# Transposing P by DMA instead of on TensorE in a two-layer recurrent attention and SwiGLU kernel

## The chip, the core and the metric

The kernel runs on one core of a Trainium2 chip. The metric is the device time of one execution in microseconds, taken over several runs as a median. Beside the runs stands one profiled execution, whose trace gives the start and length of every instruction and DMA on the core.

## What is computed

Four blocks run one after another on x (2048 x 576, bfloat16), with the same weights in both layers:

```python
x = x + A(layernorm(x)); x = x + B(layernorm(x))
x = x + A(layernorm(x)); x = x + B(layernorm(x))

def A(x, mem0, Wq, Wk, Wv, Wo, seg_len):      # 32 heads of 128, M = 8, seg_len = 32
    mem = mem0
    for s in range(n_seg):                     # 64 segments, one after another
        h = concatenate([mem, xs])             # 8 + 32 = 40 rows
        q, k, v = h @ Wq, h @ Wk, h @ Wv
        p = softmax(where(mask, q @ k.T * scale, -1e9))
        o = (p @ v) @ Wo
        mem = o[:, :M]; outs.append(o[:, M:])
    return concatenate(outs)

def B(x, w1, w3, w2):                          # 576 -> 4608 -> 576
    return (silu(x @ w1) * (x @ w3)) @ w2
```

Each segment needs the memory rows that the segment before it produced, so A is a chain of 64 steps.

## The kernel before

The two layers are interleaved: step t works on segment t of the first layer and segment t - 8 of the second (LAG = 8). There are 72 steps. The first and last eight have one layer only; the 56 between have both, and there the columns of both layers (2 x 40 = 80) go through TensorE together. The feed-forward part runs on groups of four segments, 18 weight blocks to a group, between the instructions of the attention.

A step has four groups of eight heads. A group's path is: QK and its tail QKt (queries and keys into PSUM, copied out to the tile QKT), SC (scores), the softmax on VectorE and ScalarE (add the mask, row maximum, subtract, exp, sum, reciprocal) in the tile SME, sm_pb (line 1000), which writes the normalised P into the tile PB, TR (ptr, line 1015), which transposes P of eight heads by eight matmuls against a selection matrix into two PSUM banks, PTe (pt_ev, line 1027), which copies the two banks into the tile PTS on ScalarE or VectorE, PV (line 1033), which multiplies V with PTS, an eviction into the tile OT, and WO with its tail WOt. PB has two buffers, PTS one. After a transpose GpSimd clears PB (pb_zero, line 1009), since sm_pb writes only parts of it. With both layers PB holds 104 rows (first layer in rows 0 to 39, second in 64 to 103).

The order of the work is made when the program is built. make_nodes (line 232) creates nodes with an engine, a duration, dependencies and the buffers that they take and free. plan (line 76) then places them. TensorE's order is written out by hand in strings of letters: ORDER = FIRST + FOUR * 11 + LAST, where FOUR is four steps with both layers. For the other engines plan takes, at each moment, the ready node that can start first, and among these the one with the lowest prio. A node of engine "DMA" goes to SP's queue (lines 599 to 600), "SWD" to GpSimd's, and "AD" to ScalarE or VectorE, whichever is free first. Each engine issues in exactly this order.

The letters: Q and q are QK and QKt, S is SC, T is TR, P is PV, O and o are WO and WOt, F and f the feed-forward's up-projection and its tail, W and w its down-projection for the two layers, G and g the value projection of a group and its tail, V, v, X, x other value projections, n, a and b the transposes behind the layer norms, p the transpose of the attention's output, m that of the first memory.

Each TensorE node also has tiling modes in which it can run: "full" (128 x 128), "col" (the weights in two halves of 64 columns, side by side), "row" (64 rows, two side by side) and a few smaller ones. A node with "full/col" runs in whichever of the two is set. plan adds SWITCH to a node that changes the mode. In "col" the helper mm (line 586) splits each matmul into two halves.

The weights of the feed-forward come from memory for each group anew: W13 (four DMAs, shown as tile W) and W2C (one DMA), each with two buffers, all from SP's queue. The layer norms write the normalised rows into XN, with the last 64 columns a second time behind them, so that five whole 128-column blocks can be transposed (ln_tr, line 774).

All TensorE instructions are recorded under line 591, ScalarE's under 594, VectorE's under 597 and SP's DMAs under 600, because helpers issue them.

Of the kernel before, what the change touches and what calls it, by code (L numbers as in the profile page):

```python
# [29 lines left out]
R_HT = 6  # L30

SWITCH = 0.098
# [43 lines left out]
def plan(nodes, pools, letters):  # L76
# [42 lines left out]
    while len(order) < len(nodes):  # L119
# [74 lines left out]
def ewh(*ns):  # L194
# [5 lines left out]
    "amQQQQqqqqSSqqQQQTSQqqSxXVvPTPTOPOOTooPoOoQQqqqqQSQvqqSVQQqTqSQPQOSToPXTOPTxoPOOooQqqqQQSVvqQQSQqqqQSqTQPOSTPTOP"  # L200
    "OToooPaOoQQqqqqQQSvSVQqqqQQQSqTPSXTOPTOPoTxoPOOooQQpQqqqvVqSnQQSFfqFQqfqqQTQSPFTfSOFPWOToPFToffPOOooWQqqqqQQSQQS"
    "FFfqfVvqTQWQqSFxffqQFPSXTWfPFTOPOTOPFOooooWQfqqqQQSFqfqVvQQSFfqTQPWQSqqfFTQOSfoPFTOPWFTOPooffOoFQqqQqqvSQQWSVqqf"
    "FQQWqqSTQPQSTOPabOTXPooTOPxxOooXqqpQQQqqSQnVvfSFTQqqqQQPSFffqQFTOPoSWTFfPOOTFPWOooofQQqfqqFSQFqqfgQGWTQPQSfqFQQq"
    "fqFSWTGFSggfGPGTOPOTfgFaPOOooooWVvqqfQQFFQSqfqQWQSqqfFQTQQqfqSFPWTSFPOTfoOPFWTOPffFOoooWQQqqqqQSbQQQqgqSGSTGPQTq"
    "gqQPOggSGTGPOTOPoooOoQqqqpQVpSQnQvqqqQnQFSTffqFQQPqSwTFPSffOOWTFPFTOPWOoooowFffqqQQQWSfqqFQwQSFqfqgGTQQPWfqSTFFg"
    "gfqGQwPGTOoSPFgfOGTOPWOoooFqqfqQQQQvSwqVSFqqfQQWwTFPQfqfqFTQSwPWSfFOTFPWwOTffFPOOaooooWQQqqqqQwSbQGQgqqSQTQPQqqg"
    "SGTSGPGggTOPOTOPoooOo"
# [5 lines left out]
LAST = (  # L213
    "QqqqpQQQSnpQQqqqVSvTSnQFffqPFOQqTwPoSWTFPffFTOOWPwOoooFFqfqQQQqqfSQQwQfqqFTSGSqfgQFPWQgfqGTSFPGFTfggOOPGTOPwWOoo"
    "ooFFqffqQQwQWQSqqVSvqqQQTFQPSfqqQwTOWSPFTFPofOTOPwOoooWFfqfqQQQQqfqSFwWvVSFTfqqQQPWQqqSvTQVSPOTbOPwOTooPoxOoXqQp"
    "pVvQqqqQSQQnqqSQnqQFTSfqQPFTSOPfTFOPwTOPWOooooFqfqfQQQSVqqqvQQQwSfqFWTFPSfqqQTQOPSFTwfFPOTOPWOooooFfqqQQQSqfxvVX"
    "qfFQwWTSQFQqqqfQPWSTwFPffqQFTWSOwFPffOFTOPwOooooWFvqfqQQQSWqqVQwSFfqqfQFTQQSqqWPQTPSOoTOPwOToobPxOoXqqqQQQpvSVqQ"
    "qQSnqQFfSTQFPqqfQOTSFfPwTOoofPFTOPFOfoowQqqQFSQfqqqQQSVvqqfQFTQFSfqPQOTowPSFTfxXPOTOPFOooowVvqqQQQSqqfQQSqqfQFST"
    "QQPwqqFTSOfPFTOfPwTOPfoooOoFQQqqqqQSQQSqqQVvSfTFPqQQwqfTSFPOTOFPTOPfoooOoFpwnfffFFwFwfffFFFwfffFFwFwfffFFFwfffFF"
    "wFwfffFFFfww"  # L220
# [11 lines left out]
def make_nodes(em, nseg, pools, o=Opt, dma_bw=230e3, load_bw=400e3):  # L232
# [44 lines left out]
    def ln_nodes(tag, src, xn, deps, prio, writes, warm=False):  # L277

        a = node("DVE", 1.16, em.ln_stats(src, xn), deps=deps, prio=prio, acq=[] if src is xn else [xn], name=tag + "stats")
        p_ = node("POOL", 0.45, em.ln_pow(xn), deps=[a], prio=prio, name=tag + "pow")  # L280
        c = node("DVE", 0.46 if src is xn else 0.66, em.ln_norm(src, xn), deps=[p_], prio=prio, name=tag + "norm")
        b = Slot("bank", users=len(writes))
        d = node("PE", 5 * 0.056, em.ln_tr(xn, b, warm), deps=[c], prio=prio, mode="full/col", acq=[b], rel=[xn], name=tag + "tr")
# [26 lines left out]
    def v_nodes(name, t, k, prio, tail_at, emit, strips, deps, tail_deps, free):  # L310
# [3 lines left out]
        m_ = node("PE", 8 * 0.2158, emit(b, False), deps=deps, prio=prio, mode=modes[0], acq=b, name=name)  # L314
# [40 lines left out]
    def step(t):  # L355
# [17 lines left out]
        for g in range(NG):  # L373
# [30 lines left out]
            pe_ = [node("AD", ew(4 * c80), em.pt_ev(t, g, m, bt[m], pts), deps=[tr], prio=pf, rel=[bt[m]], name="PTe") for m in (0, 1)]  # L404
# [163 lines left out]
class Emitter:  # L568
# [116 lines left out]
    def load_xn(self, g, xn):  # L685
        return lambda n: (self.dma if g else self.adma)(self.T.XN[:, xn.i, 0:D], self.a.x[g * P:(g + 1) * P, :])
# [52 lines left out]
    def init_mem(self, li, t):  # L739
        co = M_AT[self.kind(t, li), role(t)]  # L740
        return lambda n: self.v("tensor_copy", self.ht(t)[:, :, co:co + MEM], self.T.mem0T[:])


    def src_ap(self, src):
        return self.T.XN[:, src.i, 0:D] if src.pool == "xn" else self.T.XR[:, src.i, :]
# [17 lines left out]
    def ln_norm(self, src, xn):  # L763
        def f(n):
            L = self.T.LNS[:, xn.i]
            self.v("tensor_scalar", self.T.XN[:, xn.i, 0:D], self.src_ap(src), L[:, 12:13], L[:, 15:16],
                   op0=ALU.subtract, op1=ALU.mult)
            self.v("tensor_copy", self.T.XN[:, xn.i, D:D + R64], self.T.XN[:, xn.i, D - R64:D])
# [245 lines left out]

    def ptr(self, t, g, pb, b):

        def f(n):
            nq = self.nq(t)
            e = role(t) if nq == SW else 0
            sel = self.T.ident[0:104, R64 * e:R64 * e + QW]  # L1020
            if nq == SW:
                sel = bass.AP(sel.tensor, sel.offset, [list(v) for v in sel.ap][:1] + [[R64, 2], [1, QW]])
            for j in range(GH):
                self.mm(self.bk(b[j // 4])[:, (j % 4) * nq:(j % 4 + 1) * nq], self.T.PB[0:104, pb.i, j, :], sel, True, True)
        return f

    def pt_ev(self, t, g, m, b, pts):
        def f(n):
            w = 4 * self.nq(t)
            self.cp(n, self.T.PTS[:, pts.i, m * w:(m + 1) * w], self.bk(b)[:, 0:w])  # L1030
# [162 lines left out]
    def fin_cast(self, xr, xn):  # L1193
        return lambda n: self.act(self.T.XN[:, xn.i, 0:D], self.T.XR[:, xr.i, :], ACT.Copy)

    def store(self, g, xn, last):
        return lambda n: (self.dma if last else self.swdma)(self.a.out[g * P:(g + 1) * P, :], self.T.XN[:, xn.i, 0:D])
# [7 lines left out]
def kernel(  # L1205
# [39 lines left out]
    T.ident = sp.tile([P, P + QW], BF, name="ident")  # L1245
# [5 lines left out]
    T.mem0T = sp.tile([P, 5, MEM], BF, name="mem0T")  # L1251
# [12 lines left out]
    T.YTS = sp.tile([P, 2, 5, P], BF, name="YTS")  # L1264
    T.W13 = sp.tile([P, pools["w13"], NCH, 2 * P], BF, name="W13")
# [10 lines left out]
    nc.gpsimd.tensor_copy(T.ident[:, P:P + QW], T.ident[:, 0:QW])  # L1276
# [55 lines left out]
```

## Time and profile before

| | us |
|---|---|
| median of 3 runs | 2678.95 (2677.48 to 2689.47) |
| span of the profiled execution | 2684.2 |
| of it TensorE / VectorE / ScalarE / GpSimd busy | 2621.2 / 2111.8 / 1346.4 / 332.2 |
| one period FOUR (four steps) in the middle | 156.35 |

The profiled execution's own time is its span, from the first to the last instruction; nothing of it outside the span is recorded. It lies 5.2 us above the median of the runs. Matmuls overlap in TensorE, so the length of one (about 200 ns for 80 columns) is not its price; the distance from the start of one group of matmuls to the start of the next is.

### The profile page before, as it was taken

The page shows a single profiled execution, that of the slowest core. Times are in us where ns is not written, and L with a number is a line of the kernel's source. Part 1 is how long each engine was busy: PE and PEld are TensorE (multiplying, and loading weights), DVE is VectorE, ACT ScalarE, POOL GpSimd, SP SyncE. Part 2 cuts the span into 40 slices and gives each one's busy share as a digit, 9 for nine tenths or more (in the row PEclk, how much of TensorE's full clock was granted, in tenths as well). Part 3 has the DMA queues.
Part 4 walks back from the last instruction along what each step waited for, and adds up shares of the span by engine and source line. Part 5 has one row for each costly group of instructions (what it writes and reads, how often), then busy time and mean ns, then how long its engine had stood idle before and what let it go on. Part 6 is the DMA issues. An engine that isn't in the chain of part 4 may idle for free.

```text
span 2684.2 us, 136846 instructions
## 1 busy us (share of the span) xinstructions
PE 2621.2 (98%) x60881; PEld 2292.9 (85%) x60933; DVE 2111.8 (79%) x5485; ACT 1346.4 (50%) x3916; POOL 332.2 (12%) x400
## 2 busy tenths in 40 slices
PE   5999999999999999999999999999999999999998
PEld 4888888889888888988888898888889888888887
DVE  4787887887888778787877878787787878687876
ACT  2655554454545455454544545454454545455453
POOL 1111110110111011011101101110110111011110
PEclk8999999999999999999999999999999999999999
DMA  9064524344342434434333443423344342334457
GB/s 319 4 178 118 166 72 125 97 120 118 99 127 84 114 99 119 118 100 126 88 112 97 120 118 100 126 87 113 98 120 118 102 126 82 114 98 130 125 169 256
DMA packets 478178, 322.08 MB, mean 120 GB/s; under 512 B 26024, under 2 KB 467760, under 8 KB 476944
## 3 DMA queue, kind: packets, MB, share of 16 engines
q1 hardware_dynamic: 474048, 305.43, 38.7%
q8 instruction: 477, 7.82, 1.2%
q0 software_dynamic: 3024, 6.93, 0.9%
q10 hardware_dynamic: 512, 0.94, 0.2%
q14 instruction: 117, 0.96, 0.1%
HBM read 308.49 MB, written 2.36 MB: 116 GB/s over the span
## 4 chain that ended last, share of the span: by engine, by line
PE 89%; DMA 3%; DVE 3%; ACT 3%; issue 1%; SPq 1%; ACTq 0%; DVEq 0%
PE bank L591 89%; ACT V L594 1%; SPq L600 1%; DMA W<-in_B_w_dram 1%; DMA W<-in_A_Wk_dram 1%; DVE STAT L597 1%; DVE SME L597 0%; DMA WO<-in_A_Wo_dram 0%; DVE V L597 0%; DVE HTT L597 0%; DVE PB L597 0%; DMA XN<-in_A_x_dram 0%; ACT SME L594 0%; DVE PTS L597 0%; ACT PTS L594 0%
## 5 line engine op out<-in xcount | busy, mean ns | idle before, releaser
L591 PEld LDWEIGHTS <-W 128*128 128x128 bf16 (+2 forms) x32064 | 1267.3, 100 | 118.8 <-issue 55.7
L591 PE MATMUL bank<-HT,W 128*128 128x80 bf16 (+3 forms) x23040 | 807.0, 197 | 14.9 <-ACT HT L594 5.7
L591 PE MATMUL bank<-XTB,W 128*64 128x256 bf16 (+5 forms) x9024 | 664.3, 263 | 4.6 <-DMA W<-in_B_w_dram 3.1
L594 ACT ACTIVATE QKT<-bank 128x256 bf16<-128x256 f32 (+2 forms) x1477 | 343.2, 314 | 362.1 <-PE bank L591 334.1
L1010 POOL MEMSET PB<- 128x1024 bf16 x288 | 273.9, 951 | 1888.4 <-PE bank L591 1537.4
L591 PE MATMUL bank<-OT,WO 128*128 128x80 bf16 (+3 forms) x11520 | 410.9, 198 | 4.6 <-issue 2.0
L591 PEld LDWEIGHTS <-WO 128*128 128x128 bf16 (+1 forms) x11520 | 381.4, 102 | 30.4 <-issue 17.7
L594 ACT ACTIVATE V<-bank 32x512 bf16<-32x512 f32 (+1 forms) x594 | 335.8, 585 | 110.9 <-PE bank L591 104.5
L591 PE MATMUL bank<-WV,HT 128*32 128x512 bf16 (+4 forms) x3628 | 366.2, 383 | 5.5 <-issue 3.2
L591 PE MATMUL bank<-W2C,HTT 128*64 128x288 bf16 (+1 forms) x3040 | 320.1, 287 | 0.8 <-DMA W2C<-in_B_w_dram 0.4
L597 DVE TENSOR_REDUCE STAT<-SME 104x8 f32<-104x320 f32 (+1 forms) x576 | 274.6, 477 | 18.2 <-ACT SME L594 12.4
L597 DVE TENSOR_TENSOR PB<-SME,STAT 40x128 bf16<-40x128 f32 (+4 forms) x912 | 274.9, 335 | 11.3 <-POOL PB L1010 0.5
L594 ACT ACTIVATE HTT<-bank 128x512 bf16<-128x512 f32 (+1 forms) x324 | 177.6, 557 | 196.8 <-PE bank L591 195.5
L591 PEld LDWEIGHTS <-HT 128*32 128x32 bf16 (+4 forms) x3680 | 158.1, 99 | 120.3 <-issue 17.9
L591 PEld LDWEIGHTS <-HTT 128*64 128x64 bf16 (+1 forms) x3104 | 229.4, 104 | 32.1 <-issue 0.6
L597 DVE CAST QKT<-bank 128x128 bf16<-128x128 f32 (+4 forms) x571 | 154.5, 317 | 123.4 <-PE bank L591 122.4
L597 DVE SCALAR_TENSOR_TENSOR XR<-bank,XR 128x288 f32<-128x288 f32 x576 | 239.6, 446 | 13.8 <-PE bank L591 10.9
L597 DVE SCALAR_TENSOR_TENSOR HTT<-HTT,bank 128x512 bf16<-128x512 bf16 (+1 forms) x324 | 202.1, 624 | 56.1 <-ACT HTT L594 51.8
L594 ACT ACTIVATE OT<-bank 128x320 bf16<-128x320 f32 (+1 forms) x425 | 157.0, 405 | 169.5 <-PE bank L591 165.5
L597 DVE TENSOR_TENSOR HTT<-HTT,bank 128x512 bf16<-128x512 bf16 (+1 forms) x324 | 203.6, 628 | 29.0 <-PE bank L591 1.4
L594 ACT ACTIVATE PTS<-bank 128x320 bf16<-128x320 f32 (+1 forms) x395 | 148.2, 404 | 132.3 <-PE bank L591 95.7
L594 ACT ACTIVATE SME<-SME 104x320 f32<-104x320 f32 (+1 forms) x288 | 135.3, 470 | 153.4 <-DVE SME L597 151.1
(61 smaller groups left out, 1837.7 us busy)
## 6 DMA issues: line engine op xcount, KB each, us to landing
W<-in_B_w_dram SPq DMA_DIRECT2D x612, 256.0 KB, 3.7
W2C<-in_B_w_dram SPq DMA_DIRECT2D x306, 288.0 KB, 3.3
W<-in_B_w_dram SPq DMA_DIRECT2D x612, 32.0 KB, 3.3
W<-in_B_w_dram SPq DMA_DIRECT2D x8, 1024.0 KB, 10.5
W<-in_A_Wq_dram SPq DMA_DIRECT2D x9, 512.0 KB, 9.7
WO<-in_A_Wo_dram SPq DMA_DIRECT2D x4, 1152.0 KB, 17.7
XR<-in_A_x_dram POOLq DMA_DIRECT2D x16, 288.0 KB, 3.4
WV<-in_B_w_dram SPq DMA_DIRECT2D x4, 1152.0 KB, 11.3
```

Source lines behind the costliest of these rows:

```text
L591: self.ch("PE", self.nc.tensor.matmul(out, lhsT=lhsT, rhs=rhs, start=start, stop=stop, skip_group_check=True, **k))
L594: self.ch("ACT", self.nc.scalar.activation(*a, **k))
L597: self.ch("DVE", getattr(self.nc.vector, fn_)(*a, **k))
L600: self.ch("SP", self.nc.sync.dma_start(out=out, in_=in_))
L1010: return lambda n: self.ch("POOL", self.nc.gpsimd.memset(self.T.PB[:, pb.i], 0.0))
```

## The change

- In the steps with both layers, TR is no longer eight matmuls and two copies. It is one DMA that transposes rows 0 to 111 of PB (PTR = 112) for eight heads into PTS, issued from SP's queue. The planner counts 1.25 us in the queue and 1.7 us until the result can be used. PTS is laid out for 112 columns a head, and PV picks its 80 columns out of it.
- In the steps with one layer, TR stays on TensorE.
- The transposes behind the layer norms take two column halves each (mode "col" only); the second copy of the last 64 columns and its VectorE instruction are gone. XN, ident and mem0T take less memory.
- The three strings are new, and plan has a price for each pair of modes.

```diff
+PTR = 112
-SWITCH = 0.098
+SWITCH = 0.1
+SWITCHES = {"full col": 0.104, "full row": 0.107, "row full": 0.105, "row col": 0.106, "col full": 0.128, "col row": 0.14}
@@ plan
-                dur += SWITCH
+                dur += SWITCHES.get(f"{mode[0]} {n.mode[0]}", SWITCH) if mode else SWITCH
@@ FIRST, LAST: other strings
...
 FOUR = (
-    "QvqqpQQpQqqVSSnnQQFqfqfFQTQfqqWSFPwTFPSfOOTFPwTOPWOooooFffqqQQQQqqSWFSFffqgGQTQPQQgqqqGSwTFPGSfgfgFTGOPOWTOPwOoo"
-    "ooFqqQQQQqfqVvSSwWFfqfqQQTFWQwQSFffqqFPWTOPSowTFPffOTOFPWwOoooFqqfqQQQWQSqqqaQSQQbQqgqSGTSGPgTGPOTggOPGTOPwOoooo"
+    "QQppQqqqqQvVSnnSQFqqfqQQFSqffQPFwOSPWFoffPOFOWwPFOoooFfqfqQQQQqqSWGSFqqfgQQQPQgqqwSGSFPGffggFWGPOwOFPOOoooowVqfq"
+    "vQQQQqfqWSFSFfqqqQQwWQFPfqfSFwQOPSWFoFPffOOWPwOoooFqqfQQWQSqqqQQaSbQQqgqqGSQgPGSGPGggOPOwOPoooOo"
 )
@@ make_nodes, ln_nodes
-        c = node("DVE", 0.46 if src is xn else 0.66, em.ln_norm(src, xn), ...
+        c = node("DVE", 0.43 if src is xn else 0.6, em.ln_norm(src, xn), ...
-        d = node("PE", 5 * 0.056, em.ln_tr(xn, b, warm), ..., mode="full/col", ...
+        d = node("PE", 5 * 0.056, em.ln_tr(xn, b, warm), ..., mode="col", ...
@@ make_nodes, step
-            bt = banks()
-            tr = node("PE", 8 * mm80, em.ptr(t, g, pb, bt), deps=[pbs], prio=pf + o.tr, mode="full/col", acq=[pts] + bt, name="TR")
+            if nl == 2:
+                tr = node("DMA", 1.25, em.ptr_dma(t, g, pb, pts), deps=[pbs], prio=pf - 0.02, acq=[pts], name="TR", lat=1.7)
+            else:
+                bt = banks()
+                tr = node("PE", 8 * mm80, em.ptr(t, g, pb, bt), deps=[pbs], prio=pf + o.tr, mode="full/col", acq=[pts] + bt, name="TR")
             node("POOL", 1.2, em.pb_zero(pb), deps=[tr], prio=pf, rel=[pb], name="pbz")
-            pe_ = [node("AD", ew(4 * c80), em.pt_ev(t, g, m, bt[m], pts), ...) for m in (0, 1)]
+            pe_ = [tr] if nl == 2 else [node("AD", ew(4 * c80), em.pt_ev(t, g, m, bt[m], pts), ...) for m in (0, 1)]
@@ Emitter
     def ln_norm(self, src, xn):
...
-            self.v("tensor_copy", self.T.XN[:, xn.i, D:D + R64], self.T.XN[:, xn.i, D - R64:D])
     def ln_tr(self, xn, b, warm=False):
...
             for c in range(5):
-                self.mm(self.lnps(b)[:, c, :], self.T.XN[:, xn.i, c * P:(c + 1) * P], self.T.ident[:, 0:P], True, True, is_transpose=True)
+                for r in (0, R64):
+                    c0 = min(c * P + r, D - R64)
+                    self.mm(self.lnps(b)[r:r + R64, c, :], self.T.XN[:, xn.i, c0:c0 + R64], self.T.ident[:, 0:P], True, True,
+                            is_transpose=True, tile_position=(0, r))
+    def ptr_dma(self, t, g, pb, pts):
+        def f(n):
+            e, q = ("SP", self.nc.sync) if n.by == "DMA" else ("ACT", self.nc.scalar)
+            self.ch(e, q.dma_start_transpose(out=self.T.PTS[:, pts.i], in_=self.T.PB[0:PTR, pb.i].rearrange("p h n -> p (h n)")))
+        return f
     def pv(self, t, g, pts, b):
         def f(n):
             nq = self.nq(t)
+            e = role(t)
             for j in range(GH):
+                if nq == SW:
+                    x = self.T.PTS[:, pts.i, j, R64 * e:R64 * e + QW]
+                    x = bass.AP(x.tensor, x.offset, [list(v) for v in x.ap][:1] + [[R64 * (1 - 2 * e), 2], [1, QW]])
+                else:
+                    x = self.T.PTS[:, pts.i].rearrange("p h q -> p (h q)")[:, j * QW:(j + 1) * QW]
                 self.mm(self.bk(b[j // 4])[...], self.T.V[...],
-                        self.T.PTS[:, pts.i, j * nq:(j + 1) * nq], True, True)
+                        x, True, True)
@@ tiles
-    T.XN = sp.tile([P, pools["xn"], D + R64], BF, name="XN")
+    T.XN = sp.tile([P, pools["xn"], D], BF, name="XN")
-    T.PTS = sp.tile([P, pools["pts"], GH * 2 * QW], BF, name="PTS")
+    T.PTS = sp.tile([P, pools["pts"], GH, PTR], BF, name="PTS")
...
```

More of the change, by code (lines that the diff above doesn't have):

```diff
@@ L280, in ln_nodes @@
         p_ = node("POOL", 0.45, em.ln_pow(xn), deps=[a], prio=prio, name=tag + "pow")
-        c = node("DVE", 0.46 if src is xn else 0.66, em.ln_norm(src, xn), deps=[p_], prio=prio, name=tag + "norm")
+        c = node("DVE", 0.43 if src is xn else 0.6, em.ln_norm(src, xn), deps=[p_], prio=prio, name=tag + "norm")
         b = Slot("bank", users=len(writes))
-        d = node("PE", 5 * 0.056, em.ln_tr(xn, b, warm), deps=[c], prio=prio, mode="full/col", acq=[b], rel=[xn], name=tag + "tr")
+        d = node("PE", 5 * 0.056, em.ln_tr(xn, b, warm), deps=[c], prio=prio, mode="col", acq=[b], rel=[xn], name=tag + "tr")
         out = []
@@ L313, in v_nodes @@
         b = banks()
-        m_ = node("PE", 8 * 0.2158, emit(b, False), deps=deps, prio=prio, mode=modes[0], acq=b, name=name)
+        m_ = node("PE", 8 * 0.2158 + 0.11, emit(b, False), deps=deps, prio=prio, mode=modes[0], acq=b, name=name)
         n = node("PE", 0.2158, emit(b, True), deps=deps + tail_deps, prio=prio + tail_at, mode=modes[1], acq=b, name=name + "t")
@@ L1028, in f @@
         def f(n):
[L1029 to L1030 removed]
+            w = 4 * QW
+            self.cp(n, self.T.PTS[:, pts.i].rearrange("p h q -> p (h q)")[:, m * w:(m + 1) * w], self.bk(b)[:, 0:w])
         return f
@@ L1193, in fin_cast @@
     def fin_cast(self, xr, xn):
-        return lambda n: self.act(self.T.XN[:, xn.i, 0:D], self.T.XR[:, xr.i, :], ACT.Copy)
+        return lambda n: self.act(self.T.XN[:, xn.i, :], self.T.XR[:, xr.i, :], ACT.Copy)
     def store(self, g, xn, last):
-        return lambda n: (self.dma if last else self.swdma)(self.a.out[g * P:(g + 1) * P, :], self.T.XN[:, xn.i, 0:D])
+        return lambda n: (self.dma if last else self.swdma)(self.a.out[g * P:(g + 1) * P, :], self.T.XN[:, xn.i, :])
 class Tiles:
@@ L1243 @@
     T.WO = wp.tile([P, H, D], BF, name="WO")
-    T.ident = sp.tile([P, P + QW], BF, name="ident")
+    T.ident = sp.tile([P, P], BF, name="ident")
     T.maskb = sp.tile([P, 2, QW], BF, name="maskb")
```

48 lines of the change are left out of this document (20 added, 28 removed).

## The prediction

> **What bounds the kernel now.** I read the page first: span, busy times, chain.
>
> ```profile
> span 2684.2 us, 136846 instructions
> PE 2621.2 (98%) x60881; PEld 2292.9 (85%) x60933; DVE 2111.8 (79%) x5485; ACT 1346.4 (50%) x3916; POOL 332.2 (12%) x400
> ...
> PE 89%; DMA 3%; DVE 3%; ACT 3%; issue 1%; SPq 1%; ACTq 0%; DVEq 0%
> ```
>
> TensorE is busy 98% of the span and carries 89% of the chain that ended last. The program repeats one string of letters, FOUR, eleven times, so next come the stretches of one period (four steps with both layers).
>
> ```profile
> 1155.43:1311.78 156.35, 155.62 (x3468) 137.45 (x3472) 125.12 (x323) 79.16 (x229) 18.53 (x23) 1.00 0.38 109
> ...
> 1286.00:1296.00 10.00, 10.00 (x271) 9.07 (x269) 9.31 (x29) 5.85 (x26) 0.55 (x1) 1.00 0.02 4
> 1296.00:1306.00 10.00, 9.82 (x179) 7.30 (x178) 9.30 (x23) 7.81 (x18) 2.85 (x3) 1.00 0.01 3
> ```
>
> The columns are length, then PE, weight load, VectorE, ScalarE and POOL, the granted clock, the DMA share and GB/s. A period is 156.35 us, of which TensorE works 155.62 at full clock. So the time is TensorE's instruction stream, and an edit is worth what it takes out of that stream, less any wait it opens. The last step of a period (1286 to 1306) has no weight traffic, but VectorE is busy 9.3 of 10 us there.
>
> TensorE overlaps instructions, so the price of a letter is the distance from its start to the start of the next one. The timeline of PE gives it:
>
> ```profile
> 1234.46 1.92 PE L591 MATMUL bank<-XTB,W 128*64 128x256 bf16 x32
> 1236.31 5.40 PE L591 MATMUL bank<-HT,W 64*128 64x80 bf16 x152
> ...
> 1251.94 1.92 PE L591 MATMUL bank<-XTB,W 128*128 128x256 bf16 x16
> 1253.69 1.14 PE L591 MATMUL bank<-W2C,HTT 128*128 128x288 bf16 x8
> ...
> 1269.21 0.50 PE L591 MATMUL bank<-PTS,V 128*64 128x80 bf16 x16
> 1269.65 0.61 PE L591 MATMUL bank<-XTB,W 64*128 64x256 bf16 x8
> 1270.19 1.32 PE L591 MATMUL bank<-OT,WO 128*128 128x80 bf16 x32
> ...
> 1294.18 0.38 PE L591 MATMUL bank<-WV,HT 128*64 128x512 bf16 x1
> ...
> 1295.91 0.47 PE L591 MATMUL bank<-ident,PB 104*64 104x80 bf16 x15
> ...
> 1305.22 1.67 PE L591 MATMUL bank<-WV,HT 128*128 128x512 bf16 x7
> 1306.73 0.45 PE L591 MATMUL bank<-ident,PB 104*128 104x80 bf16 x8
> 1307.02 1.31 PE L591 MATMUL bank<-OT,WO 128*128 128x80 bf16 x32
> 1308.17 0.45 PE L591 MATMUL bank<-PTS,V 128*128 128x80 bf16 x8
> 1308.45 1.15 PE L591 MATMUL bank<-W2C,HTT 128*128 128x288 bf16 x8
> 1309.44 2.00 PE L591 MATMUL bank<-OT,WO 128*128 128x80 bf16 x64
> ```
>
> T (transpose of P, out of PB) 1306.73 to 1307.02: 0.29 us. O 1.15, P 0.28, W 0.99. F 1251.94 to 1253.69: 1.75. G with whole weights 1305.22 to 1306.73: 1.51; G in column halves 1294.18 to 1295.91: 1.73. A change of tiling mode: F in halves, then q, 1.85 - 1.75 = 0.10; P in halves, then f, 0.44 - 0.28 = 0.16. I take 0.12. Two f and a change 0.54, so f, and by the same token g and S, about 0.22.
>
> **TensorE's part.** What is removed, by the groups kept apart by shape:
>
> ```profile
> L591 PE MATMUL bank<-ident,PB 104*128 104x80 bf16 x1296 | 73.6, 200 | 0.0
> L591 PE MATMUL bank<-ident,PB 104*64 104x80 bf16 x992 | 30.6, 200 | 0.0
> L594 ACT ACTIVATE PTS<-bank 128x320 bf16<-128x320 f32 x301 | 123.4, 436 | 106.4 <-PE bank L591 74.7 <-DVE XR L597 13.1 <-ACT HTT L594 10.4
> L597 DVE CAST PTS<-bank 128x320 bf16<-128x320 f32 x147 | 70.6, 480 | 12.4 <-PE bank L591 8.9 <-ACT V L594 2.7
> L1010 POOL MEMSET PB<- 128x1024 bf16 x288 | 273.9, 951 | 1888.4 <-PE bank L591 1537.4 <-DVE STAT L597 261.5 <-DVE SME L597 38.4
> L597 DVE COPY XN<-XN 128x64 bf16<-128x64 bf16 x64 | 11.6, 182 | 2.2
> ```
>
> 1296 whole transposes and 992 halves are 1296 + 496 = 1792 = 224 T letters of eight heads. The letter strings say the same: 288 T before, 64 after, every other letter as often. The saving is 224 x 0.29 = 65.0 us.
>
> Two items give some back. By the plan's rule (stay in a mode while the next letter allows it) I count 1125 changes of mode in the whole old order and 1194 in the new: 69 x 0.12 = 8.3 us. And G falls into column halves 90 times instead of 55: 35 x (1.73 - 1.51) = 7.7 us.
>
> The norm transposes now always run in column halves.
>
> ```profile
> 1164.19 0.23 PE L591 MATMUL bank<-ident,XN 128*64 128x128 bf16 x1
> ...
> 1164.92 2.47 PE L591 MATMUL bank<-HT,W 128*128 128x80 bf16 x64
> ...
> 1287.64 0.45 PE L591 MATMUL bank<-ident,XN 128*128 128x128 bf16 x5
> 1287.93 1.31 PE L591 MATMUL bank<-HT,W 128*128 128x80 bf16 x32
> ```
>
> Whole, one costs 0.29; in halves, two and the change behind them take 0.73, so 0.31 each: nothing over 64 of them. The 64 copies of 0.18 us on VectorE that go with it are off the path.
>
> Sum on TensorE: 65.0 - 8.3 - 7.7 = 49.0 us. From the span, 2684.2 - 49.0 = 2635.2 us, if nothing waits.
>
> The 448 evictions of P (301 on ScalarE, 147 on VectorE) go too. They are off the path in all but the last step; there VectorE gets back the casts that it did, 0.48 each. I count nothing for it.
>
> **The new wait.** PTS has one buffer. So P of one group must end, the transpose of the next group must be issued and land, and then the next P may start. Call L the time from issue to landing. No transpose by DMA is in this trace, so L is bounded by the nearest rows (KB each, us to landing):
>
> ```profile
> W2C<-in_B_w_dram SPq DMA_DIRECT2D x306, 288.0 KB, 3.3
> ...
> W<-in_A_Wq_dram SPq DMA_DIRECT2D x9, 512.0 KB, 9.7
> ...
> out_dram<-XN SPq DMA_DIRECT2D x1, 144.0 KB, 1.8
> ```
>
> ```profile
> DMA to landing us min/median/max: 2.0/3.4/5.9
> ```
>
> The last line is that of tile W in the same period. A transpose reads 112 x 1024 bf16, 224 KB. The only transfer on this queue that starts in SBUF, the last store, lands in 1.8; the nearest in size and queue is W2C, 3.3; behind other loads it may be 5.9; behind the bulk load at the start, 9.7. I take 3.3 and keep 1.8 and 5.9 as ends.
>
> [...]
>
> Distances from the end of one P to the next, added up from the prices above over the new FOUR: within the steps the tight ones are 4.2 (FwOS), 3.6 (WFoff), 4.0 (ffOOW), 3.7 (GSG), 3.6 (GggO) and 3.3 (OwO); all others are 4.9 or more. With about 0.2 for the hand-over the need is L + 0.2 = 3.5: one distance is short, by 0.2.
>
> The other bound runs from S through the softmax on VectorE to P:
>
> ```profile
> 1266.07 0.19 PE L591 MATMUL bank<-QKT 128*64 128x40 bf16 x1
> 1296.44 0.22 PE L591 MATMUL bank<-QKT 128*64 128x40 bf16 x2
> ```
>
> ```profile
> 1269.58 1.11 DVE L597 TENSOR_TENSOR PB<-SME,STAT 40x128 bf16<-40x128 f32 x4
> ...
> 1305.13 1.06 DVE L597 TENSOR_TENSOR PB<-SME,STAT 40x320 bf16<-40x320 f32 x3
> ```
>
> From the end of S to the end of PB is 4.4 us in the first group (1266.26 to 1270.69) and 9.5 in the second (1296.66 to 1306.19), which lies in the stretch where VectorE is full; there the old order did not need it earlier. In the new order the smallest distances from S to P are 8.9, 9.1, 9.2 and 9.6. Against 4.4 + 3.3 = 7.7 nothing waits; a group that takes 6 waits up to 0.4. I put both kinds of wait at 0.7 us a period, and there are 14 periods' worth of such steps (56 steps): 10 us.
>
> SP: the transposes enter the queue of the weight loads, and a W or W2C load behind a transpose waits until PB is ready. F is who would wait for that.
>
> ```profile
> SPq L600 <- PE bank L591: 1849.2, 746, 74.5
> ```
>
> SP stands 1849 us of the span waiting for TensorE to free a weight buffer, so 224 more issues fit, and I count nothing; if that cover were gone, each would cost F up to one issue of W. POOL's clearing of PB (0.95 us) now waits for the landing, not for T; PB has two buffers, and the softmax of the group after next stands between, so it hides unless L is over 4.
>
> Forecast: 2635.2 + 10 = 2645 us as a span. The runs shown have the median 2678.95, 5.2 us under this profiled execution, so in their measure 2640 us, 1.5% less.
>
> **Rivals.** A measurement of this kernel can tell 0.5% from no change: under 2665.6 is faster, over 2692.3 slower.
>
> First, on the other side: L is 4.5, because the transpose is slower than a copy or stands behind loads in its queue. The need is 4.7, and the six tight distances fall short by 0.5, 1.1, 0.7, 1.0, 1.1 and 1.4, which is 5.8; S to P adds about 1.3 in the group with 9.1. That is 7.1 x 14 = 99 us on 2635, so 2734 as a span, 2729 as a median. It decides from L = 4.0: there the same sum is 2.9 + 0.6 = 3.5 a period, 49 us, the whole gain. For it speak the 5.9 among the W rows and that the DMA engines are 38% busy; against it, that three of the six tight places lie in the step whose DMA share is 0.01 to 0.02, where nothing stands ahead.
>
> Second: VectorE becomes the bound in the last step of a period. If PB there stays at 8 us after S, P comes at 8 + 3.3 = 11.3 where 9.2 were planned: about 2.2 us a period, 31 us, so 2666 as a span, 2661; with L at 3.7 it is 2668. For it speaks 9.3 of 10 us busy; against it, that the casts of PTS leave that stretch.
>
> Third: the heads are transposed one after another, so slowly that the queue is the bound, as 9.7 of the bulk row. Then twelve distances of a period, 58 us together, each need 9.9: 61 us short, and the four first groups some 19 more; 80 x 14 = 1120, about 3750 us. Nothing in 288 KB landing in 3.3 speaks for it.
>
> That the transposes stay on TensorE can't be: the node is one for the DMA engine whenever both layers run.
>
> **How the numbers follow.** Forecast 0.55 (all faster), VectorE 0.17 (half faster, half same), long landing 0.24 (its beginning, 0.03, same; the rest slower), queue bound 0.04. Faster 0.55 + 0.09 = 0.64, same 0.08 + 0.03 = 0.11, slower 0.21 + 0.04 = 0.25. The range starts at 2622 (L 1.8, no wait, 0.10 for a change of mode, and a few us of the old order's own waits gone) and reaches to 2725, most of the first rival; some 0.15 lies outside. The forecast's own range is 2622 to 2660.
>
> **What would show it.** Right: 64 T letters left, a period of 151 to 153 us with TensorE busy in nearly all of it, transposes that land in 3 to 3.5 us, and next to no wait of P for PTS. Wrong: P waiting for the DMA of PTS several us a period (first rival), or the transposes waiting late for PB with VectorE full from S on (second). A period over 156 would break the forecast; one under 150 would mean that mode changes cost less than I counted.

## The result, and the profile after

The changed kernel takes 2663.11 us (median of 4 runs, 2656.83 to 2664.48), the kernel before beside it 2680.48: ratio 0.9923 with the interval 0.9902 to 0.9945. A repetition, below, gives 0.9934 (0.9921 to 0.9948). So it is faster, by 0.7 to 0.8% where 1.5% was forecast: the sign is right, the gain is half the size. The profiled execution (2656.83 us) has a span of 2654.8, where the forecast had 2645; it is the shortest of the four, the next takes 2662.79.

The page of the changed kernel: span, busy times, chain, and the DMA queues (packets, MB, share of 16 engines' span).

```profile
span 2654.8 us, 132820 instructions
...
PE 2575.9 (97%) x58915; PEld 2224.6 (84%) x58915; DVE 2040.2 (77%) x5241; ACT 1229.2 (46%) x3648; POOL 334.7 (13%) x399
...
q1 hardware_dynamic: 681920, 356.84, 53.3%
q8 instruction: 460, 7.54, 1.2%
...
PE 83%; DMA 8%; DVE 5%; SPq 2%; ACT 1%; issue 1%; POOL 0%; ACTq 0%; DVEq 0%; POOLq 0%
```

TensorE lost 45.3 us of work (2621.2 to 2575.9), the span only 29.4. TensorE's part of the chain fell from 89 to 83%, and DMA's rose from 3 to 8%. The tile view of PTS and the waits say which DMA; the first row is the transpose as SP issues it (ns that it holds SP's queue: least, median, longest), the second its time from issue to landing, the others who waited for it (us in total, times, longest).

```profile
L1024 SPq DMA_TRANSPOSE PTS<-PB x224: 1222/1238/2910, 245.7 to 2359.4; - x112
...
DMA to landing us min/median/max: 2.9/3.1/5.7
```

```profile
PE bank L594 <- DMA PTS<-PB: 18.9, 29, 1.4
...
PEld L594 <- DMA PTS<-PB: 18.0, 23, 1.7
```

A transposition lands in 3.1 us at the median, as forecast (3.3), but in up to 5.7. Matmuls of P waited for it 29 times and their weight loads 23 times, up to 1.7 us.

Where the time went is read from three stretches: up to the first period, the eleven periods FOUR, and what is behind them. The rows are the last two stretches, before and then after (length, busy PE, weight load, VectorE, ScalarE and POOL, the clock that TensorE was granted, DMA share, GB/s).

```profile
529.89:2250.16 1720.27, 1711.60 (x38149) 1511.39 (x38193) 1376.24 (x3553) 870.88 (x2509) 202.96 (x241) 1.00 0.38 108
2250.16:2684.21 434.05, 420.62 (x10231) 362.58 (x10231) 330.80 (x852) 212.39 (x620) 53.61 (x62) 1.00 0.49 146
```

```profile
522.47:2211.69 1689.22, 1669.71 (x36630) 1457.37 (x36630) 1322.36 (x3377) 773.07 (x2289) 206.32 (x242) 1.00 0.56 135
2211.69:2654.80 443.11, 423.62 (x10052) 358.88 (x10051) 329.41 (x837) 203.46 (x595) 52.52 (x60) 0.98 0.54 150
```

The table sets them beside what the letters give: T letters gone x 0.29, less the changes of mode that the prediction's count adds there x 0.12 (33 in the first stretch, 33 in the periods, 3 behind).

| stretch | T gone | by the letters | measured | missing |
|---|---|---|---|---|
| up to the periods | 32 | -5.3 | -7.4 | -2.1 |
| eleven periods | 176 | -47.1 | -31.1 | 16.0 |
| behind them | 16 | -4.3 | +9.1 | 13.4 |
| sum | 224 | -56.7 | -29.4 | 27.3 |

The prediction's count of mode changes isn't quite the plan's own: run on both kernels, plan makes 1089 and 1164 (33 more in the first stretch, 44 in the periods, 2 fewer behind), because the 32-column tiles of V are a mode of their own. By it the periods should have given 45.8 and the last part 4.9, so 15 and 14 us are missing there; the table keeps the prediction's count.

So 27 us have to be explained, 16 in the periods and 13 in a last part that became slower though it lost work. This holds for one profiled execution of each kernel, and the two lie on opposite sides of their medians: by the medians the gain is 17 us (20 in the repetition) and not 29.4, so some 10 us more are missing, which the stretches can't place. The first stretch is the least certain: in the kernel before it takes 529.9 us, and with the norm halves alone (the last experiment), which only add to it, 524.5. In this execution and a second one a period takes from 151.9 to 156.5 us; before, all took 156.3 to 156.5.

### The profile page after: what moved, and what is told of

Same layout as the page of the kernel before. It is cut to its first block, busy times and chain, and to the rows that moved or that the text cites. A ratio compares the mean times of both kernels' runs of the same rounds, so it can differ in the third digit from the quotient of the medians.

```text
span 2654.8 us, 132820 instructions
## 1 busy us (share of the span) xinstructions
PE 2575.9 (97%) x58915; PEld 2224.6 (84%) x58915; DVE 2040.2 (77%) x5241; ACT 1229.2 (46%) x3648; POOL 334.7 (13%) x399
## 3 DMA queue, kind: packets, MB, share of 16 engines
q8 instruction: 460, 7.54, 1.2%
## 4 chain that ended last, share of the span: by engine, by line
PE 83%; DMA 8%; DVE 5%; SPq 2%; ACT 1%; issue 1%; POOL 0%; ACTq 0%; DVEq 0%; POOLq 0%
PE bank L594 83%; DMA PTS<-PB 5%; SPq L603 1%; DVE STAT L600 1%; DVE V L600 1%; DVE HTT L600 1%; DVE PB L600 1%; DMA W<-in_B_w_dram 1%; DMA W<-in_A_Wk_dram 1%; DVE SME L600 1%; ACT V L597 1%; DMA WV<-in_A_Wv_dram 0%; DVE XR L600 0%; DMA W2C<-in_B_w_dram 0%; POOL PB L1015 0%
## 5 line engine op out<-in xcount | busy, mean ns | idle before, releaser
L594 PEld LDWEIGHTS <-W 128*128 128x128 bf16 (+2 forms) x31824 | 1253.7, 100 | 138.5 <-issue 66.4
L597 ACT ACTIVATE QKT<-bank 128x256 bf16<-128x256 f32 (+4 forms) x1557 | 358.8, 315 | 303.9 <-PE bank L594 295.3
L597 ACT ACTIVATE V<-bank 64x512 bf16<-64x512 f32 (+1 forms) x582 | 328.6, 584 | 127.3 <-PE bank L594 120.1
L594 PE MATMUL bank<-WV,HT 128*64 128x512 bf16 (+3 forms) x3960 | 376.0, 386 | 1.1 <-DVE HT L600 0.7
L600 DVE TENSOR_REDUCE STAT<-SME 104x8 f32<-104x320 f32 (+1 forms) x576 | 273.5, 475 | 16.9 <-ACT SME L597 10.5
L597 ACT ACTIVATE OT<-bank 128x320 bf16<-128x320 f32 (+1 forms) x380 | 142.8, 402 | 306.3 <-PE bank L594 304.2
L594 PEld LDWEIGHTS <-HT 128*64 128x64 bf16 (+3 forms) x3960 | 168.5, 102 | 116.3 <-issue 21.4
L600 DVE SCALAR_TENSOR_TENSOR XR<-bank,XR 128x288 f32<-128x288 f32 x576 | 245.0, 448 | 21.4 <-PE bank L594 16.5
L600 DVE CAST V<-bank 32x512 bf16<-32x512 f32 (+1 forms) x282 | 192.8, 684 | 39.2 <-PE bank L594 33.5
L600 DVE CAST QKT<-bank 128x192 bf16<-128x192 f32 (+2 forms) x491 | 133.3, 315 | 71.3 <-PE bank L594 69.5
```

The lines of the kernel that those rows point to most:

```text
L594: self.ch("PE", self.nc.tensor.matmul(out, lhsT=lhsT, rhs=rhs, start=start, stop=stop, skip_group_check=True, **k))
L597: self.ch("ACT", self.nc.scalar.activation(*a, **k))
L600: self.ch("DVE", getattr(self.nc.vector, fn_)(*a, **k))
```

## The experiments

Ratios are to the kernel before, run beside them on the same chip, with 95% intervals; edits are shown against the changed kernel unless said otherwise.

**The changed kernel again.** No edit.

> The changed kernel itself once more, beside the others of this set. All theories: 0.990 to 0.995 of the kernel before, as first measured.

Measured: 2661.77 us, ratio 0.9934 (0.9921 to 0.9948); its eleven periods 1690.6, the part behind them 445.1. The loss in both places repeats.

**The order alone undone.** The old strings, with the 224 letters T of the two-layer steps taken out.

```diff
-FOUR = ("QQppQqqqqQvVSnnSQFqqfqQQFSqffQPFwOSPWFoffPOFOWwP..."
+FOUR = ("QvqqpQQpQqqVSSnnQQFqfqfFQQfqqWSFPwFPSfOOFPwOPWO..."
```

> The transposes go by DMA, but in the old order with the 224 letters T of the two-layer steps taken out. Theory one (the one PTS buffer and the landing time set the distance that P needs from P): the old order has distances from P to P of 2.0 to 3.2 us where about 3.1 is needed, so P waits 40 to 90 us in all and the time is 1.00 to 1.02 of the kernel before. Rival (the order hardly matters, TensorE's shorter stream is the whole gain): TensorE's stream is as short as in the changed kernel, so 0.985 to 0.995.

Measured: ratio 1.0809 (1.0795 to 1.0823). Its page, its wait of P, and the eleven periods:

```profile
PE 2642.5 (91%) x58844; PEld 2280.8 (79%) x58844; DVE 2058.6 (71%) x5318; ACT 1230.5 (43%) x3571; POOL 332.5 (11%) x399
```

```profile
PE bank L582 <- DMA PTS<-PB: 173.4, 97, 5.6
```

```profile
564.41:2429.34 1864.93, 1718.84 (x36542) 1500.50 (x36542) 1325.65 (x3410) 783.98 (x2256) 203.21 (x241) 0.97 0.50 122
```

Without a new order the DMA is a loss of 8%. The cost was put too low: the stalls also cost clock. The periods' granted clock is 0.97, and TensorE is busy 66.6 us longer than in the changed kernel with 71 fewer matmuls recorded (49.1 of them in the periods).

**The old last part.** New FIRST and FOUR, and the old LAST without its 16 T of the two-layer steps.

```diff
-LAST = ("QqqqpQQQSnpQQqqqVvSSnQFqfFqPfQOwSPWfFPOOoFfooFPWO..."
+LAST = ("QqqqpQQQSnpQQqqqVSvSnQFffqPFOQqwPoSWFPffFOOWPwOoo..."
```

> The changed kernel with the old string for the last steps (its 16 letters T of two-layer steps taken out). Theory one (the new LAST string is what makes the part after the eleventh period 9 us longer than before, 443 against 434): that part takes 430 to 436 us and the whole is 8 to 14 us under the changed kernel. Rival (the bulk loads of the last feed-forward, which start when the last QK is done, set the end whatever the order is): the part stays at 440 to 445 us and the whole within 4 us of the changed kernel.

Measured: ratio 0.9978 (0.9967 to 0.9989); the part behind the periods 454.2 us, not less than 443. That is beyond both expectations. So the new letters of LAST aren't what made that part slower; the old ones are worse still once the transposes go by DMA.

**The transposes on another queue.** ScalarE issues them; SP has the weight loads to itself.

```diff
-                tr = node("DMA", 1.25, em.ptr_dma(t, g, pb, pts), ...
+                tr = node("ACT", 1.25, em.ptr_dma(t, g, pb, pts), ...
```

> All transposes are issued from ScalarE's queue instead of SP's, so they no longer stand behind the weight loads in one queue, though they share the DMA engines with them. Theory one (a transpose is late because loads stand before it in its queue): landings of 2.9 to 3.2 us nearly everywhere, P waits under 8 us in all for PTS, and 5 to 15 us under the changed kernel unless ScalarE's 224 issues of 1.24 us come in the way of evictions. Rival (the loads take the DMA engines' bandwidth, from whichever queue): landings still reach 4 to 5 us where loads run, waits of P as before, and the time within 5 us of the changed kernel or above it.

Measured: ratio 1.0766 (1.0742 to 1.0791). The tile view of PTS and P's wait:

```profile
L1024 ACTq DMA_TRANSPOSE PTS<-PB x224: 1237/1242/2456, 246.7 to 2580.1; - x112
...
DMA to landing us min/median/max: 2.9/4.2/8.1
```

```profile
PE bank L594 <- DMA PTS<-PB: 146.0, 86, 5.8
```

The median landing rises from 3.1 to 4.2 us, so a queue without loads doesn't bring a transpose past them. A reading that fits: in SP's queue no load can be issued until the transpose is out; beside a second queue, SP goes on issuing loads into the same DMA engines. ScalarE now also stands 1.24 us at each of the 224, and how the loss splits between that and the landings was not measured.

**The weight loads left out**, after the first fill of each buffer, in the changed kernel and in the one before. The feed-forward then works on stale weights; the bulk loads of its last group stay.

```diff
+            if w13.i in self.seen13:
+                return
+            self.seen13.add(w13.i)
 ...
+            if w2.i in self.seen2:
+                return
+            self.seen2.add(w2.i)
```

> The changed kernel with the loads of W13 and W2C left out after the first fill of each buffer (the feed-forward then works on stale weights). Theory one: P waits in the two-layer steps because a transpose stands in the DMA engines behind weight loads. Then the transposes land in 2.9 us nearly throughout (maximum under 3.5), P's waits for PTS fall from 37 us (18.9 and 18.0 in the changed kernel) to under 8, the eleven periods from 1689 to about 1670 us (under 152 each), and the part after them loses its half-clock stretches too, 443 to about 435. Rival: P waits because the softmax or SP hands PB over late, whatever the loads do; then the periods stay within 4 us of 1689 and landings of 2.9 us do not shorten the waits.

> Control: the kernel before with the same loads left out. TensorE bounds it and no load is waited for in the periods, so a period stays at 156.3 us (156.0 to 156.6) and the span loses at most 5 us, in the last part where TensorE waits for W. If a period loses over 1 us, the loads slow TensorE itself, and what the other kernel gains without them is not all the transposes' landing.

Measured for the kernel before: periods of 156.4 us, so the loads themselves don't slow TensorE there. Its span is 2677.3, 10.5 us shorter in the first stretch and 3.5 longer in the last part (437.6). For the changed kernel, the two stretches, the landings and P's wait:

```profile
519.90:2203.50 1683.60, 1667.10 (x36631) 1457.66 (x36630) 1322.20 (x3377) 772.42 (x2289) 206.30 (x242) 1.00 0.17 31
2203.50:2638.57 435.07, 420.64 (x10052) 357.60 (x10051) 329.56 (x837) 203.39 (x595) 52.52 (x60) 0.99 0.18 47
```

```profile
DMA to landing us min/median/max: 2.9/2.9/4.7
```

```profile
PE bank L595 <- DMA PTS<-PB: 16.5, 25, 1.6
```

The theory was that weight loads make the transposes late. In the last part 443.1 falls to 435.1, 8 of the 13 us. In the periods it explains 5.6 of 16, by one execution. P still waits 16.5 us, and transposes still take up to 4.7 us with the DMA engines 83% idle. The theory had no reason for that, and the rival (PB handed over late) none for the long landings.

**What else is in the DMA engines.** The queue table above has a row "q8 instruction": 460 packets, 7.54 MB, 16 KB each. The number fits TensorE's own program: over 58915 matmuls and as many weight loads it is 64 bytes an instruction, and the packets come about 128 matmuls apart in the mean. Set against the start of the first such packet from 1.5 us ahead of each issue onward, the landings of the kernel without loads are (195 of the 224 could be matched, worked out from the trace's DMA packets):

```
packet starts, us after issue  <0    0-0.5  0.5-1  1-1.5  1.5-2  2-2.5  2.5-3  >3
transposes                     57    30     12     5      5      21     11     54
mean us to landing             2.94  3.16   3.74   3.98   4.44   3.90   3.86   2.93
of them over 3.5 us            1     2      9      5      5      13     6      1
```

The landing time rises with the start of the packet from 2.9 to 4.4 us and falls back to 2.9 once the packet comes behind the transpose. A second queue of instructions, q14 (117 packets of 8 KB on the page), counts too: with a packet of either in flight between 1.0 and 2.9 us after the issue, 42 of 97 took over 3.5 us, without one none of 98; with q8 alone it is 40 of 91 and 2 of 104. A packet of q8 takes 1.02 us (median). A reading that fits is that the part of the transpose behind it on its DMA engine waits; why up to 1.8 us are lost and not 1.0 wasn't found. That a packet holds up another transfer is read from these rows.

**The packets moved.** Tiny matmuls at the very start, ahead of the first norm transpose: 64 of them (128 instructions, half a packet), or 24 (48 instructions).

```diff
+        self.padded = False
...
+            for _ in range(32 if not self.padded else 0):   # 12 in the second kernel
+                self.mm(self.bk(b)[:, 0:8], self.T.ident[:, 0:P], self.T.ident[:, 0:8], True, True)
+            self.padded = True
```

> The changed kernel with 64 tiny matmuls more at its very start, while TensorE waits for the first loads: 128 instructions with their weight loads, half of one packet of 16 KB in which the trace shows the instructions being fetched. Nothing else differs, the letters and the order are the same. Theory: transposes land late because a packet of instructions for TensorE runs through the same DMA engines (in the kernel without weight loads 42 of the 97 with such a packet in flight took over 3.5 us, none of the 98 without). A period is 3330 matmuls, 6660 instructions, 26.02 packets, so the packets fall on nearly the same letters in every period, and half a packet more puts them on others. Then other transposes are late than in the changed kernel (correlation of the landing times over the 224, 0.78 between two runs of the same program, falls under 0.3), P waits longer for them (by the rise of the landing time with the start of the packet, about half as much again as before), and the eleven periods take 1700 to 1712 us for 1690, ratio to the kernel before about 0.998. Rival: the landings follow the weight loads and the softmax, which stand where they stood; then the same transposes are late and the time is within 3 us of the changed kernel, 0.992 to 0.994.

> The same with 24 tiny matmuls, 48 instructions: by the same working the shift at which the packets hit the fewest tight places. Theory: P waits 5 to 8 us less in the eleven periods, 1682 to 1686 us, ratio to the kernel before about 0.990 to 0.991. Rival: 0.992 to 0.994, as the changed kernel.

Measured: over 199 transposes the landing times of the changed kernel's two executions correlate by 0.78; those of the first with the kernel shifted by 128 by 0.01, shifted by 48 by 0.25. The letters and the order are the same, the place of the packets moved, and other transposes are late: in the kernel shifted by 128, 71 of the 121 with a packet in flight take over 3.5 us and 6 of the 78 without one. So the packets decide which ones are late: this is shown. What that costs was forecast less well. Shifted by 128 the periods take 1697.4 (1700 to 1712 expected), ratio 0.9946 (0.9934 to 0.9959), an interval that still overlaps the changed kernel's; shifted by 48 they take 1693.3 (1682 to 1686 expected), ratio 0.9938 (0.9924 to 0.9952), no faster than the changed kernel. The working that was to find the best shift doesn't predict the time.

**P freed of the transpose.** P of the two-layer steps reads a constant, so the output is no longer attention. In the plan it depends on no transpose any more, and PTS is free again as soon as the transpose is done, so SP doesn't wait for P either.

```diff
-                tr = node("DMA", 1.25, ..., acq=[pts], name="TR", lat=1.7)
+                tr = node("DMA", 1.25, ..., acq=[pts], rel=[pts], name="TR", lat=1.7)
-            pe_ = [tr] if nl == 2 else ...
+            pe_ = [] if nl == 2 else ...
...
-                    x = self.T.PTS[:, pts.i, j, R64 * e:R64 * e + QW]
-                    x = bass.AP(x.tensor, x.offset, ...)
+                    x = self.T.ident[:, 0:SW]
```

> The changed kernel with P of the two-layer steps multiplying with a constant matrix instead of PTS (so its output is not attention). The transposes are issued and land as before, but nobody in these steps waits for them. Theory: all that the change lost in the eleven periods is P waiting for late transposes. Then a period falls to the 150.7 us that the smallest distance at each letter adds up to (1658 us for eleven, 31 less than the changed kernel), and TensorE's granted clock does not fall. Rival: the change made TensorE's stream itself dearer than the letters say (changes of mode, weight loads); then the eleven periods stay above 1675.

Measured: the eleven periods, and in them TensorE's longest waits, of matmuls and of weight loads:

```profile
522.63:2201.15 1678.52, 1667.19 (x36620) 1457.99 (x36631) 1322.61 (x3377) 772.68 (x2289) 206.32 (x242) 1.00 0.57 136
```

```profile
PE bank L594 <- DMA W<-in_B_w_dram: 5.2, 6, 1.5
...
PEld L594 <- DMA W<-in_B_w_dram: 7.8, 10, 1.8
```

The same in the changed kernel's periods:

```profile
PE bank L594 <- DMA PTS<-PB: 13.5, 21, 1.4
...
PE bank L594 <- DMA W<-in_B_w_dram: 0.3, 1, 0.3
...
PEld L594 <- DMA PTS<-PB: 16.0, 21, 1.7
PEld L594 <- DMA W<-in_B_w_dram: 0.5, 1, 0.5
```

The periods fall by 10.7 us, a third of the 31 expected, and at 1678.5 they stay above the 1675 that was to mark the rival, a dearer stream. Against the rival speaks where the rest stands. A wait takes the place of part of the old one: TensorE's wait for the feed-forward's weights rises from 0.3 to 5.2 us by the matmuls. With that taken off, 1678.5 - 5.2 = 1673.3 us are left, and the letters give 1720.3 - 47.1 = 1673.2 (1674.5 by the plan's own count of modes). So no sign is left that the stream is dearer than the letters say, to within a few us, since the wait of the weight loads (7.8 us) overlaps that of the matmuls and isn't counted (in the changed kernel's trace 14.9 of the 18.2 us that weight loads wait for W lie within the matmuls' waits for W). Of the 16 us missing, 10.7 go when P is freed of the transposes; that the other 5 are a wait for weights which P's wait had covered is the reading that fits. The 1658 expected was a sum of the smallest distance at each letter, which no period reaches.

**Loads split, transpose first.** Each W13 load as two nodes, and TR ahead of everything that SP can issue.

```diff
-                tr = node("DMA", 1.25, ..., prio=pf - 0.02, acq=[pts], name="TR", lat=1.7)
+                tr = node("DMA", 1.25, ..., prio=pf - 100, acq=[pts], name="TR", lat=1.7)
-                    ld = [node("DMA", kb(1152, 256) / dma_bw, em.load_w13(pr_, w13), ...)]
+                    ld = [node("DMA", kb(576, 256) / dma_bw, em.load_w13(pr_, w13, kind), ...) for kind in (0, 1)]
```

> The changed kernel with each W13 load split into two nodes of two DMAs, and TR given first place among what SP can issue. Theory one (P waits for transposes behind weight loads): less stands ahead of a transpose, its longest landings fall from 4.6 to about 4, P's waits for PTS from 37 us to about 20, and the time falls by 5 to 12 us against the changed kernel, ratio to the kernel before about 0.989. Rival (what stands ahead of the transpose was issued long before it, so the order in the queue matters little): within 3 us of the changed kernel, 0.992 to 0.994.

Measured: ratio 0.998 (0.9972 to 0.9989), periods 1701.4; neither side expected that. The median landing is 3.2, the longest 5.2, and both waits of the periods rise:

```profile
PE bank L594 <- DMA PTS<-PB: 17.1, 29, 1.8
PE bank L594 <- DMA W<-in_B_w_dram: 5.2, 9, 1.0
```

So the order of SP's queue matters after all: with the transposes first, weights come late, and the transposes don't come earlier. Which of the two edits did it isn't known.

**G on whole weights.**

```diff
-        m_ = node("PE", 8 * 0.2158, em.vg(t, g, b, False), deps=deps, prio=t + o.vm, mode="full/col", acq=b, name="VG")
+        m_ = node("PE", 8 * 0.2158, em.vg(t, g, b, False), deps=deps, prio=t + o.vm, mode="full", acq=b, name="VG")
```

> The changed kernel with G, the value projection, always on whole weights instead of whichever mode is set. It makes 103 changes of mode more (about 11 us by the plan's own 0.104 to 0.128 each) and moves 90 G out of column halves. By the prediction's prices (G whole 1.51, in halves 1.73) that is 11.1 - 90 x 0.22 = 8.7 us less than the changed kernel, ratio to the kernel before about 0.990. Rival: the 1.51 was read from a group with one matmul record missing from the trace, both modes cost about 1.73, and only the changes of mode are left: about 11 us more than the changed kernel, ratio about 0.997.

Measured: ratio 1.0046 (1.0032 to 1.006), 0.011 to 0.012 above the changed kernel, on the rival's side and beyond it. The timeline of PE in this kernel, G whole:

```profile
1202.30 1.90 PE L594 MATMUL bank<-WV,HT 128*128 128x512 bf16 x8
1204.13 0.40 PE L594 MATMUL bank<-QKT 128*64 128x40 bf16 x15
```

From its start to the next, with a change of mode: 1.83, so 1.72 for G. In halves it was 1.73. The distances whose own or next mode changed add up to 9.9 us over the eleven periods, with 88 changes of mode more: 0.11 each, as the plan and the prediction had it. The other 19.8 of the periods' 29.7 us are waits that came with the new times: 10.0 of them at one place, two q with a wait for VectorE between them, and 6.5 at one where P waits.

**The norm halves alone**, on the kernel before.

```diff
-        d = node("PE", 5 * 0.056, em.ln_tr(xn, b, warm), ..., mode="full/col", ...
+        d = node("PE", 5 * 0.056, em.ln_tr(xn, b, warm), ..., mode="col", ...
-            self.v("tensor_copy", self.T.XN[:, xn.i, D:D + R64], self.T.XN[:, xn.i, D - R64:D])
...
-                self.mm(self.lnps(b)[:, c, :], self.T.XN[:, xn.i, c * P:(c + 1) * P], ...)
+                for r in (0, R64):
+                    self.mm(self.lnps(b)[r:r + R64, c, :], self.T.XN[:, xn.i, c0:c0 + R64], ...)
```

> The kernel before with the norm transposes in column halves and without the copy that goes with them, nothing else. The prediction put this part at nothing on TensorE and nothing for the 64 copies. Theory one: within 0.2% of the kernel before (45 changes of mode more in the old order, about 5 us at 0.11 each, ratio 1.000 to 1.002). Rival: VectorE's copies in front of the transposes were on the path, and it is faster by up to 64 x 0.18 = 11.6 us, ratio down to 0.996.

Measured: ratio 1.0019 (1.001 to 1.0028), periods 1725.7 for 1720.3: 5.4 us for 33 changes of mode more. The copies were off the path. In the median the kernel is 5 us slower, which is what some 45 changes of mode cost at 0.11; the periods of this one execution, 0.16 a change, lie a little above that. What this part does beside the new order wasn't tried.

## Why the prediction was right, and where half the gain went

**TensorE's part** holds: 64 T left, 65.0 us out, changes of mode at 0.11 to 0.12. One term was wrong: G in column halves was to give back 35 x (1.73 - 1.51) = 7.7 us, and gives back nothing. The 1.51 came from a row with x7 where G has eight matmuls: the trace lacks the first, and the distance was taken from the second. In the changed kernel's timeline a whole G stands complete:

```profile
1203.18 1.89 PE L594 MATMUL bank<-WV,HT 128*128 128x512 bf16 x8
1204.90 0.45 PE L594 MATMUL bank<-PTS,V 128*128 128x80 bf16 x8
```

1.72. So the stream was to fall by 56.7, not 49.0, and the forecast came as near as it did by luck: this error hid part of the next. (The count of mode changes, 69 for the plan's 75, is worth 0.7 us.)

**The new wait** is the step that failed: 0.7 us a period, 7.7 over the eleven. By the distance between letters, less the smallest at the same letter in six kernels with this FOUR, the changed kernel loses 27.6 us in its eleven periods, and 23.1 of them at the letter just ahead of P. Counted from the letters' sum instead, 16 are missing, 10.7 of which go when P is freed. By either count the wait is two to three times the 7.7. The mechanism was the first rival's (a transpose behind other traffic), but not its size: L was right at the median, and the error was to take it as one number. It ranges from 2.9 to 5.7, and distances up to about 5 are tight for some of the transposes. The six distances named as tight are therefore not the places of the waits: WFoff loses 6.5 us and GggO 2.8, the other four next to nothing, while OwOF, 5.3 us long, loses 2.9. Ahead of a P that comes over 20 us after the last one, 2.3 us are lost; its transposes were issued 0.06 us after PB was written (median), so there the path from S through the softmax sets the time, the prediction's other bound. What makes L long was in no step of the prediction. Packets of TensorE's own instructions do in part (shown by shifting them); the weight loads do in part (5.6 us of the periods when left out). The prediction's 0.2 for the hand-over was an estimate worked out from no row; in the changed kernel it is 0.08 us from the end of a P to the issue of the next transpose (median of the 97 issued within 0.15 us of it) and 0.05 from a landing to the matmul of P that waited for it (median of 29).

**SP**, at which nothing was counted, isn't free.

```profile
SPq L603 <- PE bank L594: 907.1, 627, 75.5
SPq L1024 <- DVE PB L600: 405.5, 129, 16.5
```

Its wait for TensorE fell from 1849 to 907 us, and another 405 us now stand ahead of a transpose whose PB isn't ready, with weight loads queued behind. With P freed, the wait for those weights is what comes next; with the loads gone, the packets of instructions still make P wait. So taking one away saves 10.7 or 5.6 us, not the 16.

**The last part**, which had no step of its own, loses 13.4 us. Its timeline and the windows at the two places:

```profile
2584.76 0.35 PE L594 MATMUL bank<-QKT 128*40 128x40 bf16 x7
2588.02 0.22 PE L594 MATMUL bank<-QKT 128*40 128x40 bf16 x1 [2.91 <-issue]
...
2640.69 4.10 PE L594 MATMUL bank<-XTB,W 64*128 64x128 bf16 x36 [4.99 <-DMA W<-in_B_w_dram]
```

```profile
2585.00:2592.00 7.00, 4.09 (x82) 2.33 (x81) 3.05 (x9) 1.59 (x6) 0.00 (x0) 0.61 1.06 344
2634.00:2654.80 20.80, 11.22 (x125) 8.89 (x122) 8.13 (x20) 2.60 (x6) 0.00 (x0) 0.83 0.24 78
```

Two gaps, 2.91 and 4.99 us, and with each the granted clock is down: 0.61 over 7.00 us and 0.83 over 20.80, which is at most (0.39 x 7.00) + (0.17 x 20.80) = 6.3 us. In the kernel before, the wait for the same weights at the end is 2.5 us, and the clock behind it stays at 1.00:

```profile
PE bank L591 <- DMA W<-in_B_w_dram: 2.5, 1, 2.5
```

```profile
2663.00:2684.20 21.20, 14.31 (x205) 11.85 (x202) 12.02 (x30) 4.13 (x10) 0.00 (x0) 1.00 0.42 147
```

The fall begins inside each gap: the clock is 0.50 for 6.8 us from 2586.5 on and again from 2637.7 on. The length of a gap alone doesn't decide, since in the kernel before a gap of 1.45 us at the first place has a clock of 0.50 behind it (2626.90 to 2630.30), and the 2.5 above has none. No transpose by DMA runs in these gaps. Without the weight loads 8.0 us of the loss go and the wait of 4.99 us with them, while a gap of 2.4 stays at the first place (the kernel before gained nothing in this part by that), so much of it hangs on the loads. Why they come later than before isn't settled: the old letters make this part longer, not shorter. During the first gap no wait is recorded and a packet of instructions is in flight behind bulk loads (2585.58 to 2586.62, DMA share 1.06); that TensorE stood without instructions is likely, but was not tested.

**The rivals.** VectorE as the bound of the last step didn't come: the transposes there mostly land in 2.9 us, and at GggO, the one place there where more than 0.5 us is lost, PB is written 1.8 us before its transpose is issued (median). The queue as the bound (9.7) didn't come either: all eight heads land in 3.1 us at the median. "A period of 151 to 153" was met by the better periods only, and "next to no wait of P" was wrong.

No version run here that computes the same beats the changed kernel: the two shifts can't be told from it, and the split loads, G on whole weights and the old last part are slower. What is left to be had in the periods is at most the 16 us down to the 1673 of the letters.

## What to carry to other kernels

A step moved from a busy engine to a DMA must be scheduled by the long end of its landing time, not by the median: here 2.9 alone, 3.1 at the median, up to 4.7 behind a packet that no kernel line issues, and 5.7 at the longest. Add up the gain by stretches and subtract what each stretch should have given; the stretch that the change hardly touches can lose as much as the one that it was made for. And before taking a price from one row of the timeline, count its instructions.

## What the runs showed that was not expected

- The fetch of TensorE's own program, 1.2% of the DMA engines' time, lengthened the transposes by up to 1.8 us (2.9 to 4.7, with the weight loads left out). Since a period of 6660 instructions is 26.02 packets, the packets fall on nearly the same letters in every period.
- Stalls cost more than their length here: with 173 us of waits for the transposes the granted clock of the periods fell to 0.97, and TensorE's busy time in them rose by 49 us.
- A DMA transposition held the queue that issued it for 1.24 us (median), on SP and on ScalarE, and from a queue other than that of the loads it landed later (4.2 for 3.1 us at the median).
